# Attention of groups 4 to 6 one weight pair sooner, K's logarithms and exponentials in one row, and x's split held behind them

## The chip, the cores and the metric

One core of a Trainium2 chip runs the whole program in one launch. The metric is the device time in microseconds (us); lower is better. The names used below: TensorE (PE in the rows; PEld is its weight loads), VectorE (DVE), ScalarE (ACT), GpSimd (POOL), and SyncE, whose queue issues most DMAs (SPq). A few DMAs are issued from ScalarE's queue (ACTq).

## The reference

A complex linear recurrence over 768 steps, for 4 x 8 heads of 48 channels, gives the rows `x` of a mixture of four experts with ReLU; every expert sees every row.

```python
def _attn_ref(q, k, v, a_re, a_im):
    mag = np.sqrt(a_re * a_re + a_im * a_im)
    scale = np.minimum(mag, 0.999) / (mag + 1e-06)
    a_re_n, a_im_n = (a_re * scale, a_im * scale)
    for t in range(S):
        ar, ai = (a_re_n[:, :, t, :, None], a_im_n[:, :, t, :, None])
        new_re = ar * S_re - ai * S_im
        new_im = ar * S_im + ai * S_re
        kv = np.einsum('bhd,bhe->bhde', k[:, :, t], v[:, :, t])
        S_re, S_im = (new_re + kv, new_im)
        y[:, :, t] = np.einsum('bhd,bhde->bhe', q[:, :, t], S_re)
...
def _moe_ref(x, domain_probs, w1, w2):        # x: 3072 x 384, F = 1024
    p = domain_probs / (domain_probs.sum(-1, keepdims=True) + 1e-09)
    for e in range(E):
        h = np.maximum(x @ w1[e], 0.0)
        out += p[:, e:e + 1] * (h @ w2[e])
```

## The kernel before

The 3072 rows are cut into 12 groups of 256. For each group the program first normalises the decays A (`norm`: squares, a reduction, a logarithm, an exponential and some products), multiplies them up along time (`prefix`, a scan whose last rows are L376 and L377), and then makes Q and K. `head` (L487 to L508) squares the scanned A (L488, L489), reduces (L492), takes logarithm (L494) and exponential (L495) of the two token halves, and multiplies Q (L497). `tail` (L512 to L516) multiplies K. Q and K go through DRAM (`q_d`, `k_d`) into another layout (Qst, Kst), TensorE makes scores (`sc`) and `yp`, ScalarE copies `y`, and a store from ScalarE's queue puts it in DRAM (`y_d`, L704). `load_x` (L218) brings it back as `xa`.

Ahead of an expert, `split_x` (L221) cuts `xa` into a rounded high part `xha` (ScalarE, L225) and a low part `xla` (VectorE, L227). `moe1(g-1)` runs experts 0 and 1 on one group: eight weight pairs, each with a `w1_step` of 18 matmuls into `ph` (L238), ScalarE's ReLU `hh` (L249), VectorE's remainder `hl` (L250), and a `w2_step` of 12 matmuls into `po` (L261). The work of pair k stands in the names as `ph_k`, `hh_k`, `hl_k`. After the last pair of an expert, ScalarE adds `po` into `acc` (two instructions, one for each 128 rows, L743).

Below, block g is the stretch in which TensorE runs `moe1` on group g. In block g the attention of group g+1 is spread between the pairs, and `norm`, `prefix` and `head` of the groups behind it too. `stream` (L884) hands out that work in portions, `between(k)` (at L940) is called after pair k: from pair `FIRST` on it issues three steps of attention, and at the last pair it calls `split_x` for the next group (L948). `FIRST` (L60), `STEP` and `MORE` are tables written by hand.

What each engine runs is a fixed row of instructions. The scheduler of the program sets it when the program is built, by a simulated timeline; `behind(x, p)` makes x stand behind p there, and `keep_in_program_order` fixes an instruction's place among others so marked. At run time an engine works through its row from the front.

After the twelve groups a second phase runs experts 2 and 3 on other tiles. Its weights (`late_weights`) are prepared at the end of the first phase, with stores `late_d` from SyncE's queue (L793, L794).

Of the kernel before, what the change touches and what calls it, by code (L numbers as in the profile page):

```python
# [11 lines left out]
ALU = mybir.AluOpType  # L12
# [44 lines left out]
NSEL = 2  # L57
XSEL = 3
NPIN = 5
FIRST = {1: 5, 2: 5, 3: 4, 4: 4, 5: 4, 6: 4, 7: 3, 8: 3, 9: 3, 10: 3, 11: 3}  # L60
STEP = {1: 4.2, 2: 4.2, 3: 4.2, 4: 4.2, 5: 4.2}
MORE = (1.9, 1.9, 0.5)
HALF = tuple(range(2, 12))
# [59 lines left out]
def fast_path(ctx, tc, qkP, aP, vP, probsP, w, out, flag):  # L123
# [94 lines left out]
        wts["xd"] = nc.sync.dma_start(x, y_d[g].rearrange("(j p) t -> p j t", p=P))  # L218
        return [(slice(0, G), x)]

    def split_x(g, parts):  # L221
        xh = moe.tile([P, NJ, G], F32R, tag="xh", name=f"xha{g}")
        xl = moe.tile([P, NJ, G], F32R, tag="xl", name=f"xla{g}")
        for ts, x in parts:
            ins = nc.scalar.activation(xh[:, :, ts], x, AF.Copy)  # L225
            tc.keep_in_program_order(ins)
            tc.keep_in_program_order(nc.vector.tensor_tensor(xl[:, :, ts], x, xh[:, :, ts], op=ALU.subtract))  # L227
        wts["x"] = ins
        return xh, xl

# [65 lines left out]
    with ExitStack() as c1:  # L296
# [165 lines left out]
        def finish(g, A, qk):  # L462
# [24 lines left out]
            def head(lo, hi):  # L487
                nc.scalar.activation(some(a2a, lo, hi), some(A[:, 0], lo, hi), AF.Square)  # L488
                nc.scalar.activation(some(b2a, lo, hi), some(A[:, 1], lo, hi), AF.Square)  # L489
                for c in range(lo, hi):  # L490
                    a2, ic = some(a2a, c, c + 1), some(i0a, c, c + 1)
                    red = nc.vector.tensor_tensor_reduce(a2, a2, some(b2a, c, c + 1), scale=1.0, scalar=3e38,  # L492
                                                         op0=ALU.add, op1=ALU.min, accum_out=st_a2[:, c, g:g + 1])
                    nc.scalar.activation(ic, a2, AF.Ln, scale=2.0 ** A2_LOG[c], bias=a2b)  # L494
                    last_act = nc.scalar.activation(ic, ic, AF.Exp, scale=-1.0, bias=a2e[:, c:c + 1])  # L495
                for c in range(2):
                    ins = nc.vector.tensor_tensor(dst(Q[:, c, :, :C], lo, hi), rows(A[:, c], lo, hi),  # L497
                                                  rows(qk[:, 0], lo, hi), op=ALU.mult)
                    if g < NSEL and lo == 1:
                        behind(ins, red)  # L500
                        last["qp"] = ins
                if hi == CG:
                    nc.scalar.activation(Q[:, :, :, C].rearrange("p c (j n) -> p c j n", n=CG),
                                         A[:, :, SEG - 1, NS - 1::NS].unsqueeze(3).broadcast_to([P, 2, NJ, CG]),
                                         AF.Copy)
                return last_act
# [381 lines left out]
        def stream():  # L888
            for g in range(1, NG):
                if g > NSEL:  # L890
                    here = nc.sync.dma_start(here_d, Kst[0:1, 0, CG - 1, 0:1])
                    behind(here, last["q"])
                    last["q"] = here
                qk = load_qk(g, last["q"])
                if g + 1 < NG:
                    A.append(load_a(g + 1, prev=last["q"]))
                for r in front(g, A[g], qk):
                    yield g, r
                if g + 1 < NG:
                    for r in norm(g + 1, A[g + 1]):  # L900
                        yield g, r

        work = stream()
# [20 lines left out]
        for g in range(1, NG + 1):  # L924
# [7 lines left out]
            def between(k, g=g, first=first, end=end):  # L932
# [12 lines left out]
                    if k == end:  # L945
                        over.add(g)
                if k == max(end, nk - 1) and g in x and g >= NSEL:
                    x[g] = split_x(g, x[g])  # L948
                advance(STEP.get(g, 3.4) + (MORE[k - first] if first <= k <= end else 0.0), g + 1)

            moe1(g - 1, *x.pop(g - 1), between)
# [565 lines left out]
```

## Time and profile before

| | |
|---|---|
| time, median of 3 runs | 964.38 us (963.53 to 966.71) |
| the profiled execution's own time | 963.93 us |
| its span, first to last instruction | 962.2 us |
| TensorE busy | 935.6 us (97%) |
| VectorE busy | 740.6 us (77%) |
| ScalarE busy | 480.2 us (50%) |
| mean granted TensorE clock | 0.997 |

A busy share is a mean over all stages. A timeline row gives start and length of one instruction or of several alike that follow each other, and in brackets how long the engine stood idle ahead of it, with the instruction that it waited for. Lengths of neighbours overlap by a pipelining share, so that the distance of two starts is the price of an instruction in a row. A released wait names what came last.

### The profile page before, as it was taken

The page shows a single profiled execution, that of the slowest core. Times are in us where ns is not written, and L with a number is a line of the kernel's source. Part 1 is how long each engine was busy: PE and PEld are TensorE (multiplying, and loading weights), DVE is VectorE, ACT ScalarE, POOL GpSimd, SP SyncE. Part 2 cuts the span into 40 slices and gives each one's busy share as a digit, 9 for nine tenths or more (in the row PEclk, how much of TensorE's full clock was granted, in tenths as well). Part 3 has the DMA queues.
Part 4 walks back from the last instruction along what each step waited for, and adds up shares of the span by engine and source line. Part 5 has one row for each costly group of instructions (what it writes and reads, how often), then busy time and mean ns, then how long its engine had stood idle before and what let it go on. Part 6 is the DMA issues. An engine that isn't in the chain of part 4 may idle for free.

```text
span 962.2 us, 18383 instructions
## 1 busy us (share of the span) xinstructions
PE 935.6 (97%) x7037; PEld 912.9 (95%) x7037; DVE 740.6 (77%) x1640; ACT 480.2 (50%) x952; POOL 165.2 (17%) x206
## 2 busy tenths in 40 slices
PE   5899999999999999999999999999999999999997
PEld 3799999989999999999999999999999999999997
DVE  7889989988989999889895676758485757676642
ACT  7756436364464636446253455636454554444430
POOL 6020000000000000000000026333534362322000
PEclk9999999999999999999999999999999999999999
DMA  9686175674857468393949799231514443131112
GB/s 299 193 156 165 54 202 137 166 150 135 179 149 187 120 149 192 113 216 97 215 115 275 268 302 273 60 116 41 151 60 137 155 96 99 50 99 50 50 50 77
DMA packets 131459, 139.57 MB, mean 145 GB/s; under 512 B 8802, under 2 KB 115090, under 8 KB 131362
## 3 DMA queue, kind: packets, MB, share of 16 engines
q1 hardware_dynamic: 116130, 107.84, 38.9%
q0 software_dynamic: 11488, 26.93, 12.1%
q10 hardware_dynamic: 3744, 3.54, 1.4%
q8 instruction: 57, 0.93, 0.4%
q14 instruction: 40, 0.33, 0.1%
HBM read 89.80 MB, written 48.47 MB: 144 GB/s over the span
## 4 chain that ended last, share of the span: by engine, by line
PE 60%; DMA 3%; DVE 2%; ACT 1%; issue 0%; SPq 0%; DVEq 0%; ACTq 0%
PE pob L979 20%; PE pb L979 17%; PE po L261 9%; PE ph L238 9%; PE sc L604 2%; PE yp L621 1%; PE yp L626 1%; DMA RX<-w 1%; PE dp L586 1%; DMA Z<-y_d 1%; PE ktp L567 1%; DMA late_d<-lwl 0%; DMA xa<-y_d 0%; DVE lws L779 0%; DMA y_d<-y 0%
## 5 line engine op out<-in xcount | busy, mean ns | idle before, releaser
L979 PE MATMUL pob<-shi,hid 128*128 128x384 f32 x528 | 148.3, 334 | 0.0
L261 PE MATMUL po<-whi,hh 128*128 128x384 f32 x384 | 129.9, 338 | 1.4 <-ACT hh L249 1.0
L261 PE MATMUL po<-wlo,hh 128*128 128x384 f32 x384 | 128.7, 335 | 0.0
L249 ACT ACTIVATE hh<-ph 128x512 fp32r<-128x512 f32 x96 | 57.1, 595 | 132.0 <-PE ph L238 126.2
L991 POOL TENSOR_TENSOR Z<-Z 128x384 f32<-128x384 f32 x84 | 90.6, 1123 | 112.3 <-DMA Z<-y_d 47.9
L238 PE MATMUL ph<-xha,whi 128*128 128x256 f32 x576 | 103.3, 287 | 2.9 <-ACT xha L225 2.8
L238 PE MATMUL ph<-xla,whi 128*128 128x256 f32 x576 | 101.8, 284 | 0.6 <-DVE xla L227 0.6
L238 PE MATMUL ph<-xha,wlo 128*128 128x256 f32 x576 | 102.4, 284 | 0.0
L979 PE MATMUL pb<-xh,shi 128*128 128x384 f32 x291 | 97.2, 335 | 0.6 <-DVE pb L985 0.6
L979 PEld LDWEIGHTS pob<-shi,hid 128*128 128x128 f32 x528 | 96.4, 188 | 0.2 <-DVE hid L988 0.2
L979 PE MATMUL pb<-xh,slo 128*128 128x384 f32 x288 | 96.2, 334 | 0.0
L979 PE MATMUL pb<-xl,shi 128*128 128x384 f32 x288 | 96.2, 334 | 0.0
L250 DVE SCALAR_TENSOR_TENSOR hl<-ph,hh 128x512 fp32r<-128x512 f32 x96 | 66.0, 688 | 32.3 <-ACT hh L249 31.8
L238 PEld LDWEIGHTS ph<-xha,whi 128*128 128x128 f32 x576 | 85.1, 190 | 5.4 <-ACT xha L225 4.0
L979 PE MATMUL pob<-slo,hid 128*128 128x384 f32 x264 | 88.2, 334 | 0.0
L261 PE MATMUL po<-whi,hl 128*128 128x384 f32 x384 | 84.3, 336 | 0.0
L238 PEld LDWEIGHTS ph<-xla,whi 128*128 128x128 f32 x576 | 83.2, 190 | 1.1 <-DVE xla L227 0.8
L238 PEld LDWEIGHTS ph<-xha,wlo 128*128 128x128 f32 x576 | 82.7, 190 | 0.2 <-issue 0.2
L982 ACT ACTIVATE SN<-pb 128x384 f32<-128x384 f32 x96 | 47.3, 492 | 66.6 <-PE pb L979 59.2
L985 DVE TENSOR_TENSOR xl<-Z,xh 128x384 fp32r<-128x384 f32 x104 | 60.1, 607 | 21.1 <-ACT xh L982 13.3
L261 PEld LDWEIGHTS po<-whi,hh 128*128 128x128 f32 x384 | 72.4, 189 | 2.2 <-ACT hh L249 1.4
L982 ACT ACTIVATE hid<-pb 128x384 fp32r<-128x384 f32 x76 | 37.3, 490 | 72.3 <-PE pb L979 71.7
(227 smaller groups left out, 2069.6 us busy)
## 6 DMA issues: line engine op xcount, KB each, us to landing
qk<-qkP SPq DMA_DIRECT2D x24, 384.0 KB, 3.6
acc_d<-acc POOLq DMA_DIRECT2D x24, 384.0 KB, 4.8
ACC<-acc_d SPq DMA_DIRECT2D x48, 192.0 KB, 2.9
A<-aP SPq DMA_DIRECT2D x22, 384.0 KB, 5.5
k_d<-K SPq DMA_DIRECT2D x40, 192.0 KB, 4.1
Kst<-k_d SPq DMA_DIRECT2D x40, 192.0 KB, 5.7
Z<-y_d SPq DMA_DIRECT2D x16, 384.0 KB, 3.9
q_d<-Q SPq DMA_DIRECT2D x24, 193.5 KB, 3.7
```

The lines of the kernel that those rows point to most:

```text
L238: ins = nc.tensor.matmul(ph[:, u, :], wt[:, j * P:(j + 1) * P], xt[:, j, :], start=(n == 0), stop=(n == 3 * NJ - 1))
L249: wts["hh"] = nc.scalar.activation(hh, ph, AF.Relu)
L250: wts["hl"] = nc.vector.scalar_tensor_tensor(hl, ph, 0.0, hh, op0=ALU.max, op1=ALU.subtract)
L261: ins = nc.tensor.matmul(po[t], part[0][:, u, t * P:(t + 1) * P], wts[i][n][:, HD:], start=(i % FE == 0 and part[0] is hh and n == 0), sto ...
L567: ins = nc.tensor.transpose(kt_ps[:, j * P:(j + 1) * P], K[0][:, i, j * CG + c, :], ident)
L586: ins = nc.tensor.matmul(d_ps[o:o + n, h, :], KT[:, h, o:o + n], vc[:, h * D:(h + 1) * D], start=True, stop=True)
L604: ins = nc.tensor.matmul(s_ps[:, h, :], Kc[:, hf * 4 + h, :], Qc[:, hf * 4 + h, :], start=True, stop=True)
L621: ins = nc.tensor.matmul(yo, st[:, o:o + n], Qc[:, o // D, :], start=True, stop=False)
L979: return tc.keep_in_program_order(nc.tensor.matmul(*args, **kw))
L982: return pin(nc.scalar.activation(dst, src, fn, scale=scale))
L985: pin(nc.vector.tensor_tensor(dst, x, y, op=op))
L991: nc.gpsimd.tensor_tensor(dst, x, y, op=op)
```

## The change

Four things are changed. `FIRST` goes from 4 to 3 for groups 4, 5 and 6. In `head`, for groups above 2, the logarithm of the second half is held behind the exponential of the first, so that exponential, logarithm and exponential stand in one row. The norm of the next group (its squares and its reduction) is held behind the last exponential and the last K product for these groups. And `split_x` for groups from 3 on is held: `xha` behind the last exponential, `xla` behind the last Q product that have been issued.

```diff
--- before.py
+++ after.py
@@ -57,7 +57,7 @@
 NSEL = 2
 XSEL = 3
 NPIN = 5
-FIRST = {1: 5, 2: 5, 3: 4, 4: 4, 5: 4, 6: 4, 7: 3, 8: 3, 9: 3, 10: 3, 11: 3}
+FIRST = {1: 5, 2: 5, 3: 4, 4: 3, 5: 3, 6: 3, 7: 3, 8: 3, 9: 3, 10: 3, 11: 3}
 STEP = {1: 4.2, 2: 4.2, 3: 4.2, 4: 4.2, 5: 4.2}
 MORE = (1.9, 1.9, 0.5)
 HALF = tuple(range(2, 12))
@@ -218,13 +218,16 @@
         wts["xd"] = nc.sync.dma_start(x, y_d[g].rearrange("(j p) t -> p j t", p=P))
         return [(slice(0, G), x)]
 
-    def split_x(g, parts):
+    def split_x(g, parts, prev=(None, None)):
         xh = moe.tile([P, NJ, G], F32R, tag="xh", name=f"xha{g}")
         xl = moe.tile([P, NJ, G], F32R, tag="xl", name=f"xla{g}")
         for ts, x in parts:
             ins = nc.scalar.activation(xh[:, :, ts], x, AF.Copy)
             tc.keep_in_program_order(ins)
-            tc.keep_in_program_order(nc.vector.tensor_tensor(xl[:, :, ts], x, xh[:, :, ts], op=ALU.subtract))
+            low = tc.keep_in_program_order(nc.vector.tensor_tensor(xl[:, :, ts], x, xh[:, :, ts], op=ALU.subtract))
+            for later, p in zip((ins, low), prev):
+                if p is not None:
+                    behind(later, p)
         wts["x"] = ins
         return xh, xl
 
@@ -491,11 +494,14 @@
                     a2, ic = some(a2a, c, c + 1), some(i0a, c, c + 1)
                     red = nc.vector.tensor_tensor_reduce(a2, a2, some(b2a, c, c + 1), scale=1.0, scalar=3e38,
                                                          op0=ALU.add, op1=ALU.min, accum_out=st_a2[:, c, g:g + 1])
-                    nc.scalar.activation(ic, a2, AF.Ln, scale=2.0 ** A2_LOG[c], bias=a2b)
+                    ln = nc.scalar.activation(ic, a2, AF.Ln, scale=2.0 ** A2_LOG[c], bias=a2b)
+                    if g > NSEL and c > lo:
+                        behind(ln, last_act)
                     last_act = nc.scalar.activation(ic, ic, AF.Exp, scale=-1.0, bias=a2e[:, c:c + 1])
                 for c in range(2):
                     ins = nc.vector.tensor_tensor(dst(Q[:, c, :, :C], lo, hi), rows(A[:, c], lo, hi),
                                                   rows(qk[:, 0], lo, hi), op=ALU.mult)
+                    last["qm"] = ins
                     if g < NSEL and lo == 1:
                         behind(ins, red)
                         last["qp"] = ins
@@ -897,7 +903,8 @@
                 for r in front(g, A[g], qk):
                     yield g, r
                 if g + 1 < NG:
-                    for r in norm(g + 1, A[g + 1]):
+                    prev = (last["act"], last["dve"]) if g > NSEL else (None, None)
+                    for r in norm(g + 1, A[g + 1], prev=prev):
                         yield g, r
 
         work = stream()
@@ -945,7 +952,7 @@
                     if k == end:
                         over.add(g)
                 if k == max(end, nk - 1) and g in x and g >= NSEL:
-                    x[g] = split_x(g, x[g])
+                    x[g] = split_x(g, x[g], (last["act"], last["qm"]) if g >= XSEL else (None, None))
                 advance(STEP.get(g, 3.4) + (MORE[k - first] if first <= k <= end else 0.0), g + 1)
 
             moe1(g - 1, *x.pop(g - 1), between)
```

The rows of the engines are the same in both kernels up to the middle of block 2. The first place shown is ScalarE at the border of block 2 and block 3. Here `xha_2417` is the split of group 3, `A_1530` group 4's decays and `A_2003` group 5's, `s`, `u` the intermediates of `head` and `norm`, `acc_1` the sum of block 2. Before:

```order
L249 ACTIVATE hh_6_2401<-ph_6_2382 128x512
L225 ACTIVATE xha_2417<-xa_2354 128x768
L249 ACTIVATE hh_7_2462<-ph_7_2443 128x512
L488 ACTIVATE s_2006<-A_1530 128x768
L489 ACTIVATE s_2006<-A_1530 128x768
L494 ACTIVATE u_2007<-s_2006,a2b 128x24x16
L503 ACTIVATE Q_2008<-A_1530 128x12
L389 ACTIVATE s_2430<-A_2003 128x768
L390 ACTIVATE s_2430<-A_2003 128x768
L249 ACTIVATE hh_0_2516<-ph_0_2497 128x512
L494 ACTIVATE u_2007<-s_2006,a2b 128x24x16
L495 ACTIVATE u_2007<-u_2007,a2e 128x24x16
```

After:

```order
L252 ACTIVATE hh_6_2401<-ph_6_2382 128x512
L252 ACTIVATE hh_7_2462<-ph_7_2443 128x512
L749 ACTIVATE acc_1_2532<-po_4_0_2208,pr 128x384
L749 ACTIVATE acc_1_2532<-po_4_1_2209,pr 128x384
L491 ACTIVATE s_2006<-A_1530 128x768
L492 ACTIVATE s_2006<-A_1530 128x768
L497 ACTIVATE u_2007<-s_2006,a2b 128x24x16
L509 ACTIVATE Q_2008<-A_1530 128x12
L500 ACTIVATE u_2007<-u_2007,a2e 128x24x16
L497 ACTIVATE u_2007<-s_2006,a2b 128x24x16
L500 ACTIVATE u_2007<-u_2007,a2e 128x24x16
L225 ACTIVATE xha_2417<-xa_2354 128x768
```

`xha` moved from behind `hh_6` to behind the two copies into `acc_1` and the whole row of group 4's `head`; `hh_7` now stands ahead of it. The squares of group 5's norm (`s_2430`) come behind it.

The second place is TensorE at the same border. `po_4` is the sum that `acc_1` copies, `whi` and `wlo` are weights. Before:

```order
L261 MATMUL po_4_0_2208<-whi_602,hl_6_2402 128x384
L261 MATMUL po_4_1_2209<-whi_602,hl_6_2402 128x384
L238 MATMUL ph_0_2497<-xha_2417,whi_502 128x256 x3
L238 MATMUL ph_0_2497<-xha_2417,wlo_503 128x256 x3
L261 MATMUL po_4_0_2208<-whi_604,hh_7_2462 128x384
L261 MATMUL po_4_0_2208<-wlo_824,hh_7_2462 128x384
L261 MATMUL po_4_1_2209<-whi_604,hh_7_2462 128x384
```

After (the fence leaves out the rest of pair 7's twelve matmuls):

```order
L264 MATMUL po_4_0_2208<-whi_602,hl_6_2402 128x384
L264 MATMUL po_4_1_2209<-whi_602,hl_6_2402 128x384
L264 MATMUL po_4_0_2208<-whi_604,hh_7_2462 128x384
...
L264 MATMUL po_4_0_2208<-whi_606,hl_7_2463 128x384
L264 MATMUL po_4_1_2209<-whi_606,hl_7_2463 128x384
L241 MATMUL ph_0_2497<-xha_2417,whi_502 128x256 x3
L241 MATMUL ph_0_2497<-xha_2417,wlo_503 128x256 x3
L241 MATMUL ph_1_2554<-xha_2417,whi_524 128x256 x3
L241 MATMUL ph_1_2554<-xha_2417,wlo_525 128x256 x3
L241 MATMUL ph_0_2497<-xla_2418,whi_502 128x256 x3
```

All twelve matmuls of pair 7's `w2_step` moved ahead of the first matmul that reads `xha`, and the first ones of `ph_1` moved up among those of `ph_0`. Behind the last `po_4` row nothing stands that does not read `xha` or `xla`.

The third place is ScalarE at the next border, of block 3 and block 4, with the split of group 4 (`xha_2981` before, `xha_3003` after). Before:

```order
L488 ACTIVATE s_2486<-A_2003 128x768
L249 ACTIVATE hh_6_2965<-ph_6_2946 128x512
L489 ACTIVATE s_2486<-A_2003 128x768
L225 ACTIVATE xha_2981<-xa_2918 128x768
L494 ACTIVATE u_2487<-s_2486,a2b 128x24x16
L503 ACTIVATE Q_2488<-A_2003 128x12
L389 ACTIVATE s_2994<-A_2483 128x768
L390 ACTIVATE s_2994<-A_2483 128x768
L494 ACTIVATE u_2487<-s_2486,a2b 128x24x16
L495 ACTIVATE u_2487<-u_2487,a2e 128x24x16
L249 ACTIVATE hh_7_3026<-ph_7_3007 128x512
L495 ACTIVATE u_2487<-u_2487,a2e 128x24x16
```

After:

```order
L252 ACTIVATE hh_5_2930<-ph_5_2911 128x512
L491 ACTIVATE s_2486<-A_2003 128x768
L492 ACTIVATE s_2486<-A_2003 128x768
L497 ACTIVATE u_2487<-s_2486,a2b 128x24x16
L509 ACTIVATE Q_2488<-A_2003 128x12
L252 ACTIVATE hh_6_2987<-ph_6_2968 128x512
L500 ACTIVATE u_2487<-u_2487,a2e 128x24x16
L497 ACTIVATE u_2487<-s_2486,a2b 128x24x16
L500 ACTIVATE u_2487<-u_2487,a2e 128x24x16
L392 ACTIVATE s_2955<-A_2483 128x768
L393 ACTIVATE s_2955<-A_2483 128x768
L225 ACTIVATE xha_3003<-xa_2883 128x768
```

Here `head` of group 5 starts ahead of `hh_6` and not around it, `xha` stands behind the exponentials and behind the squares of the next norm, and `hh_7` follows it; the copies into `acc` come later. TensorE keeps its order of the row before here: six matmuls that read `xha`, then pair 7's `po`. The borders up to that of blocks 8 and 9 look like this one, with `hh_6` up to three places earlier in the row of `head` at four of them.

At the border of blocks 10 and 11 TensorE now has eight of pair 7's `po` matmuls ahead of the first six that read `xha`, the last step of group 11's attention stands inside `ph_6` where it stood behind pair 3's `po`, and on SyncE's queue the load of `xa` stands behind the first two stores of `late_d` (L794) where it stood ahead of them.

## Rows read from the trace of the kernel before

**Rows 1.** The page's first part: TensorE's busy time, its share of the span and its instructions.

```profile
PE 935.6 (97%) x7037; PEld 912.9 (95%) x7037; DVE 740.6 (77%) x1640; ACT 480.2 (50%) x952; POOL 165.2 (17%) x206
```

**Rows 2.** The view of waits, TensorE alone: who waited for whom, microseconds in total, times, the longest.

```profile
PE qp L457 <- DVE Q L497: 2.8, 1, 2.8
PE ph L238 <- ACT xha L225: 2.8, 3, 1.6
```

**Rows 3.** The timeline of TensorE around the border of block 2 and block 3 (start us, length us, line, operation, tiles; in brackets the idle time before it and who ended it).

```profile
188.28 0.52 PE L238 MATMUL ph<-xha,whi 128*128 128x256 f32 x3
190.43 0.34 PE L261 MATMUL po<-whi,hh 128*128 128x384 f32 x1
191.82 0.86 PE L261 MATMUL po<-whi,hl 128*128 128x384 f32 x4
194.27 0.62 PE L238 MATMUL ph<-xha,whi 128*128 128x256 f32 x3 [1.59 <-ACT xha L225]
```

**Rows 4.** The timeline of ScalarE over the same border, same columns.

```profile
193.38 0.84 ACT L225 ACTIVATE xha<-xa 128x768 fp32r<-128x768 f32 x1 [4.92 <-DMA xa<-y_d]
194.13 0.58 ACT L249 ACTIVATE hh<-ph 128x512 fp32r<-128x512 f32 x1
194.60 0.84 ACT L488 ACTIVATE s<-A 128x768 f32<-128x768 f32 x1
195.34 0.83 ACT L489 ACTIVATE s<-A 128x768 f32<-128x768 f32 x1
196.81 0.62 ACT L494 ACTIVATE u<-s,a2b 128x384 f32<-128x384 f32 x1 [0.64 <-DVE st_a L492]
197.43 0.83 ACT L389 ACTIVATE s<-A 128x768 f32<-128x768 f32 x1
198.17 0.83 ACT L390 ACTIVATE s<-A 128x768 f32<-128x768 f32 x1
199.39 0.60 ACT L494 ACTIVATE u<-s,a2b 128x384 f32<-128x384 f32 x1
199.89 0.61 ACT L495 ACTIVATE u<-u,a2e 128x384 f32<-128x384 f32 x1
200.40 1.03 ACT L743 ACTIVATE acc<-po,pr 128x384 f32<-128x384 f32 x2
```

**Rows 5.** The timeline of VectorE, same columns: the reduction of group 4's norm, K of group 3, the end of group 4's norm, the last scan row of group 4, and the last scan row of group 5.

```profile
157.98 0.95 DVE L391 CUSTOM_DVE_ANT_0 s<-s 128x768 f32<-128x768 f32 x1
164.21 1.02 DVE L516 TENSOR_TENSOR K<-A,u 128x384 f32<-128x384 f32 x2
167.72 1.76 DVE L418 TENSOR_TENSOR A<-A,s 128x1536 f32<-128x1536 f32 x1
190.40 0.83 DVE L377 TENSOR_TENSOR A<-fm_1a,fm_1b 128x651 f32<-128x651 f32 x1
233.31 0.83 DVE L377 TENSOR_TENSOR A<-fm_1a,fm_1b 128x651 f32<-128x651 f32 x1
```

**Rows 6.** The view by windows (stretch, its length, busy time and count of PE, PEld, DVE, ACT, POOL, then the granted TensorE clock as a share, DMA share, GB/s) for the stretch after TensorE's wait for `qp`, the border, and the end of the program; below it the last matmul row of TensorE's timeline.

```profile
27.00:28.00 1.00, 0.84 (x10) 0.78 (x12) 0.95 (x5) 0.90 (x2) 0.00 (x0) 0.94 1.18 415
28.00:30.00 2.00, 2.00 (x22) 1.98 (x19) 2.00 (x7) 0.39 (x2) 0.00 (x0) 0.50 0.83 290
30.00:32.00 2.00, 2.00 (x17) 1.67 (x14) 2.00 (x6) 0.71 (x2) 0.00 (x0) 0.68 0.01 3
192.00:194.00 2.00, 0.68 (x4) 0.36 (x3) 0.37 (x1) 0.62 (x1) 0.00 (x0) 1.00 0.37 130
959.00:960.00 1.00, 0.00 (x0) 0.00 (x0) 0.00 (x0) 0.00 (x0) 0.00 (x0) 0.86 0.05 11
960.00:962.00 2.00, 0.00 (x0) 0.00 (x0) 0.00 (x0) 0.00 (x0) 0.00 (x0) 0.50 0.02 8
...
955.42 0.34 PE L979 MATMUL pob<-shi,hid 128*128 128x384 f32 x1
```

**Rows 7.** The timeline of TensorE at three more places in the attention blocks.

```profile
241.95 0.52 PE L238 MATMUL ph<-xla,whi 128*128 128x256 f32 x3
243.14 0.45 PE L261 MATMUL po<-whi,hh 128*128 128x384 f32 x1 [0.67 <-ACT hh L249]
329.31 0.51 PE L238 MATMUL ph<-xha,wlo 128*128 128x256 f32 x3
330.16 0.44 PE L261 MATMUL po<-whi,hh 128*128 128x384 f32 x1 [0.34 <-ACT hh L249]
342.22 0.86 PE L261 MATMUL po<-whi,hl 128*128 128x384 f32 x4
343.19 0.57 PE L604 MATMUL sc<-Qst,Kst 112*128 112x128 f32 x3
```

**Rows 8.** The timelines of ScalarE, of SyncE's DMA issues and of TensorE at the border of blocks 10 and 11: the last `y` of group 11 and its split, `xa`'s load and one store of the late weights, and block 11's first `ph`.

```profile
537.64 1.21 ACT L632 ACTIVATE y<-yp 48x512 f32<-48x512 f32 x2 [1.03 <-PE yp L626]
544.75 0.85 ACT L225 ACTIVATE xha<-xa 128x768 fp32r<-128x768 f32 x1
541.51 0.37 SPq L218 DMA_DIRECT2D xa<-y_d  x1
545.35 0.32 SPq L794 DMA_DIRECT2D late_d<-lwm  x1
550.54 0.62 PE L238 MATMUL ph<-xha,whi 128*128 128x256 f32 x3
```

## Prediction

> **What bounds the kernel now.** I read the busy shares first [rows 1]: TensorE works for 935.6 of 962.2 us, so a change pays only where it takes idle time from TensorE, and costs only where it adds some. Then the view of waits for TensorE alone [rows 2]. Among the waits on other engines after the start-up, the largest entry is `ph` waiting for `xha`: 2.8 us in three waits, and one of them, 1.6 us, is at the border of blocks 2 and 3. So I went to the timelines of that border.
>
> TensorE ends pair 6 of block 2 (the four `hl` matmuls that start at 191.82, with 0.173 us between starts, so the next could start at 192.51) and then stands until `xha` lets it start at 194.27 [rows 3]. The two starts are 1.76 us too far apart; that is the whole price of the wait, restart included. ScalarE shows why [rows 4]: `xha` starts at 193.38 after 4.92 us of idle time that `xa`'s load ends. The next row shows something else: `hh` of pair 7 runs at 194.13, right behind `xha`, though its `ph` was complete when TensorE began the following `po` matmuls at 190.43 [rows 3]. It was ready for over 3 us on an idle engine, and did not pass the `xha` ahead of it. So ScalarE's row holds at run time, and what stands ahead of `xha` in that row is paid in full.
>
> **The change part by part.** *The split of group 3.* In the changed row, `xha` of group 3 stands behind `hh_7`, the two copies into `acc_1` and the whole `head` of group 4. The copies read the sum of block 2, which is complete only when pair 7's last `hl` matmul is. So all of `head` must run after block 2's last matmul and ahead of block 3's first, and TensorE has nothing else queued there. Step by step:
>
> TensorE: pair 7's twelve `po` matmuls follow pair 6 at once, and a `w2_step` lasts 2.09 us (from 190.43 to 192.51) [rows 3]. Block 2 ends at 192.51 + 2.09 = 194.6.
>
> ScalarE: two copies, 1.03 us [rows 4], to about 195.65. Then the start of L488 to the start of the first logarithm, 2.21 us (194.60 to 196.81, with the reduction between them) [rows 4]. That logarithm and the small Q copy take 0.62 (196.81 to 197.43), and the exponential, logarithm and exponential 0.5 each (199.39 to 199.89 to 200.40) [rows 4]. `xha` thus starts at 195.65 + 2.21 + 0.62 + 1.5 = 200.0, and with its own 0.84 it ends at 200.8. From the order alone TensorE is idle from 194.6 to 200.8, 6.2 us.
>
> VectorE can only add to it. `head` needs the last scan row of group 4, which before starts at 190.40 [rows 5] and ends at 191.2. The scan now starts later: the reduction of group 4's norm, at 157.98 before, is held behind K of group 3, which ends at 165.2 [rows 5]. K comes 0.9 us sooner without that reduction ahead of it, so the reduction is up to 6.3 us later. The old way from there to the norm's last product at 167.72 has K's rows in it (the last two alone 0.9 us [rows 5]) that are now done, so I carry 4 to 5.4 us to the scan's end: 195.2 to 196.6. At the lower end the copies are later still and the idle time stays at 6.2 us; at the upper end it is 7.2. I take 6.6.
>
> With a restart of 0.16 (1.76 against the 1.59 of idle time that the row prints [rows 3]) the new wait is 6.8 us, and the old 1.76 goes: **+5.0 us**, with ends +4.6 and +5.6. `xla`, which stands behind three of K's products on VectorE, may add 0 to 0.3.
>
> *The clock behind it.* TensorE's granted clock is 1.00 through the wait of 1.59 us [rows 6], so that wait cost nothing further. After the wait of 2.8 us for `qp` [rows 2] the clock falls at about 27.9 to half (1.2 of 2.4 GHz) and is back at about 31.3, 3.4 us later [rows 6]. At the end, with the last matmul at 955.42 and nothing behind it, the clock reads full until about 959.7 and then half [rows 6]. An idle time of 6.6 us is longer than that, so I expect it to fall within the gap and the first matmuls of block 3 to run at half speed. I take 3.4 to 4 us of them, half of it lost: **+1.8 us**; ends 0 (no fall) and 2.1. At half speed the wait for `xla` is covered.
>
> The Trainium skill, page "TensorE: Matmul & The Clock Gate", section "HAM oscillation — how this bites in real kernels", says that a TensorE left waiting between bursts starts the next burst throttled, and gives 1.67 us of throttled time for each burst of its example, half of which is lost. By that figure the term would be an estimated 0.8 us and the sum 1.0 us lower. The row here measures the stretch at half clock as twice as long, and that is the one I use.
>
> *The later borders.* There the copies stand behind `xha`. From the end of `ph_6` TensorE has `po` of pair 5, `ph_7` and `po` of pair 6 ahead of it, 2.09 + 2.15 + 2.09 = 6.3 us [rows 3]. ScalarE's longest row from that point is `hh_6`, logarithm, Q copy, exponential, logarithm, exponential (2.6 us), the two squares (0.74 each [rows 4]) and `xha` (0.84), 4.9 us. So `xha` is in time by 1.4 us if the squares of `head` are done by then. At the first such border pair 6 ended at 243.14 - 0.83 - 2.15 = 240.2 before (the wait below and one `ph`) [rows 7]; 6.8 later for the new wait and 6.3 back, `ph_6` ends near 240.7. The scan of group 5 ended at 234.1 before [rows 5]; with the held norm I place it near 236, and the squares with their reduction 2.2 us behind that. The cover holds, and it grows, since `FIRST` puts the attention one pair (4.2 us) ahead.
>
> What this frees is read at three places where TensorE stood for ScalarE or for Kst in blocks 4 to 6 [rows 7]. A full `ph` row of three matmuls lasts 0.36, so 243.14 comes 0.83 too late after 241.95, and 330.16 comes 0.49 too late after 329.31; four `po` last 0.69, so 343.19 comes 0.28 too late. That is 1.6 us: **-1.6 us**, with ends 0 (each reappears elsewhere in the new row) and -2.1 (two more gaps of about 0.2).
>
> *The last border.* Group 11's attention ends about one pair later (4.2 us and some), and on SyncE's queue `xa`'s load is moved past two stores of late weights. Before, `xa` was issued at 541.51, `xha` ended at 545.6, and block 11's first `ph` started at 550.54 [rows 8], a slack of 4.9 us. TensorE's own order gives another 1.4 us (eight `po` matmuls go ahead). `y` is then late by 4.7 us with 6.3 to spend. The store that now stands ahead of `xa` was issued at 545.35 [rows 8], about when `y` lands in the new order. I cost it at nothing; if the store is later too, it costs up to 2 us.
>
> *The rest.* `FIRST` for three groups and the row of logarithms move work within engines that have idle time; no instruction is added. I cost them at nothing beyond the terms above.
>
> Sum, against the profiled execution's own time of 963.93 us: 963.93 + 5.0 + 1.8 - 1.6 = **969.1 us**. Its own time lies 0.45 us under the median of 964.38, which is inside the range.
>
> **The rivals.**
>
> *The clock does not fall.* For it: the fall at 27.9 came when TensorE had already resumed after a wait and had been half idle for some time, so that row doesn't prove that one gap does it; against it: the end of the program, where idle time alone did. Time: 963.93 + 5.0 + 0.3 - 1.6 = 967.6; with the low ends (4.6, and -2.1) 966.4, which a measurement couldn't tell from no change.
>
> *A second border comes late.* At the border of blocks 3 and 4 `head` stands ahead of `hh_6` now, so a late scan would hold `hh_6` and then `xha`; at blocks 10 and 11 it is the queue. For it: the slack of 1.4 us on ScalarE and some 1.5 us on SyncE's queue are both small. Against it: VectorE needs less than a block for a group, so the scan gains from block to block. A miss of 2 us, without another fall of the clock, gives 971.1; with one, 973.
>
> *Faster: the hold is free.* If block 2's copies and `head` ran before TensorE's row ended, the old wait of 1.76 us and the 1.6 us at the other places would go and nothing would come: 963.93 - 1.76 - 1.6 = 960.6. It decides at one point: `xha` of group 3 ends ahead of 194.6. For it: `hh_7` comes sooner by 3 us, and VectorE has spare time. Against it: the copies stand ahead of `head` in ScalarE's row, and `hh` at 194.13 shows that nothing passes there.
>
> *The change moves next to nothing.* All holds fall where the engines waited anyway: about 964. Against it stands the same row.
>
> **How the numbers follow.** Forecast (one long wait at blocks 2 and 3, clock at half behind it): 0.66, 968 to 970.5. A second late border: 0.15, 970.5 to 973. No fall of the clock: 0.14, 966 to 968. Hold free or gains larger than I see: 0.03, 960.6. Next to nothing: 0.02, 964. The range from 966.3 to 972.5 leaves out the last two, and the ends of the second and third case.
>
> A measurement of this kernel can tell about 0.3% from no change, 2.9 us: slower is over 967.3, faster under 961.5. Slower: 0.66 + 0.15 + half of 0.14 = 0.88, less a little for terms missed, 0.86. Same: 0.11. Faster: 0.03.
>
> **What would show it.** In the changed profile, the wait of `ph` for `xha` at about 194.6 should read 6 to 7 us, with two copies, `head`'s two squares, logarithm, exponential, logarithm and exponential ahead of `xha` on ScalarE's timeline; the granted clock should read 0.5 for 3 to 4 us from about 201, in windows of 2 us; the waits of `po` for `hh` in the waits view should be gone or under 0.5 us; and `ph` should not wait for `xha` again up to 586 us. I am wrong if `xha` of group 3 runs before the copies, if the wait is under 4 us, or if the clock stays at full level.

## The result, and the profile after

The changed kernel takes 973.21 us (median of 6 runs, 971.71 to 974.75) against 964.87 us for the kernel before in the same session (6 runs). The ratio is 1.0084, 95% interval 1.0069 to 1.0100: slower by 8.3 us, where I had forecast 5.2 and a range up to 972.5. The direction was right and the size was not. The profiled execution took 973.38 us, with a span of 971.6.

First the busy shares and then the waits of TensorE in the changed kernel, to be read beside [rows 1, 2]: busy time has hardly moved, so the time is in gaps.

```profile
PE 936.2 (96%) x7037; PEld 912.7 (94%) x7037; DVE 741.0 (76%) x1640; ACT 479.1 (49%) x952; POOL 165.0 (17%) x206
```

```profile
PE ph L241 <- ACT xha L225: 9.1, 5, 6.7
PE qp L460 <- DVE Q L502: 3.1, 1, 3.1
PE po L264 <- DVE hl L253: 1.3, 2, 1.0
PE sc L610 <- issue: 1.1, 1, 1.1
PE po L264 <- ACT acc L749: 0.5, 1, 0.5
```

The wait for `xha` went from 2.8 us to 9.1, and three smaller entries are of a kind that the first did not lead me to expect. TensorE's timeline at the border of blocks 2 and 3, to set beside [rows 3]:

```profile
193.62 0.86 PE L264 MATMUL po<-whi,hl 128*128 128x384 f32 x4
201.22 1.01 PE L241 MATMUL ph<-xha,whi 128*128 128x256 f32 x3 [6.75 <-ACT xha L225]
202.03 0.84 PE L241 MATMUL ph<-xha,wlo 128*128 128x256 f32 x3
203.95 0.60 PE L241 MATMUL ph<-xla,whi 128*128 128x256 f32 x3
204.38 0.52 PE L241 MATMUL ph<-xha,whi 128*128 128x256 f32 x3
```

The last of the four `po` starts at 194.14, the next matmul at 201.22: 7.08 us, 6.91 more than the usual 0.17. ScalarE's timeline over that gap, beside [rows 4]:

```profile
194.34 1.05 ACT L749 ACTIVATE acc<-po,pr 128x384 f32<-128x384 f32 x2 [3.39 <-PE po L264]
195.80 0.84 ACT L491 ACTIVATE s<-A 128x768 f32<-128x768 f32 x1 [0.41 <-DVE A L379]
198.02 0.61 ACT L497 ACTIVATE u<-s,a2b 128x384 f32<-128x384 f32 x1 [0.63 <-DVE st_a L495]
199.82 0.61 ACT L500 ACTIVATE u<-u,a2e 128x384 f32<-128x384 f32 x1
200.34 0.83 ACT L225 ACTIVATE xha<-xa 128x768 fp32r<-128x768 f32 x1
```

The two copies, the squares, the logarithms and the exponentials stand between block 2's last matmul and `xha`, in the order that the prediction read from the code. The windows of this stretch (columns as in [rows 6]):

```profile
196.00:198.00 2.00, 0.00 (x0) 0.00 (x0) 1.09 (x4) 1.39 (x2) 0.54 (x1) 0.82 0.62 58
198.00:200.00 2.00, 0.00 (x0) 0.00 (x0) 2.00 (x4) 1.95 (x5) 0.00 (x0) 0.50 0.75 138
202.00:204.00 2.00, 2.00 (x12) 2.00 (x11) 2.00 (x5) 0.64 (x1) 0.00 (x0) 0.50 0.95 247
204.00:206.00 2.00, 2.00 (x18) 2.00 (x18) 2.00 (x5) 0.35 (x1) 0.00 (x0) 0.97 0.36 104
```

The granted clock falls near 197.3 (0.82 over the two microseconds from 196) to 0.50, the 1.2 GHz level, and is back just behind 204. Of that, 2.9 us (201.22 to about 204.1) fall on matmuls, and half of it, some 1.4 us, is lost.

So far this is the forecast. The rest lies at the other end of the first phase. Timelines of VectorE, SyncE's DMA issues, ScalarE and TensorE there, beside [rows 8]: the last scan row of group 11, the last load of its `Kst`, its first `sc`, a store of late weights, `xa`'s load and split, block 11's first `ph`, a wait for `hl`, and the first matmul of the second phase:

```profile
500.71 0.83 DVE L380 TENSOR_TENSOR A<-fm_1a,fm_1b 128x651 f32<-128x651 f32 x1
529.41 1.23 SPq L539 DMA_DIRECT2D Kst<-k_d  x2
533.41 2.02 PE L610 MATMUL sc<-Qst,Kst 112*128 112x128 f32 x16 [1.10 <-issue]
550.77 0.32 SPq L800 DMA_DIRECT2D late_d<-lwm  x1
555.35 0.37 SPq L218 DMA_DIRECT2D xa<-y_d  x1
558.73 0.84 ACT L225 ACTIVATE xha<-xa 128x768 fp32r<-128x768 f32 x1 [3.14 <-DMA xa<-y_d]
559.62 0.62 PE L241 MATMUL ph<-xha,whi 128*128 128x256 f32 x3 [0.85 <-ACT xha L225]
571.52 0.97 PE L264 MATMUL po<-whi,hl 128*128 128x384 f32 x4 [1.00 <-DVE hl L253]
594.97 0.33 PE L986 MATMUL pb<-xh,shi 128*128 128x384 f32 x1
```

In the kernel before, the scan row starts at 486.25, the `sc` at 520.38, `xa`'s load at 541.51, and the second phase at 585.26. To see where the time accrues I compared TensorE's start of the same matmul in both traces. At the last `po` of block 9 the changed kernel is 3.3 us late, with six `ktp` matmuls (0.57 us) still to do that the other had behind it, so 3.9 on equal work. At the first matmul of the second phase it is 9.7 us late, and it stays so to the last matmul (+9.67). **Some 5.8 us, more than the whole net forecast of 5.2, is lost within blocks 10 and 11**, in small pieces: 1.26 at the `sc`, about 0.2 at each of five `yp`, 0.41 at `scs`, 1.01 at `xha`, 1.17 and 0.47 at `hl`, 0.67 at `acc` (start to start, less the usual step; a piece of 0.60 was there before).

### The profile page after: what moved, and what is told of

It is laid out like the page before. It is cut to its first block, busy times and chain, and to the rows that moved or that the text cites. A ratio compares the mean times of both kernels' runs of the same rounds, so it can differ in the third digit from the quotient of the medians.

```text
span 971.6 us, 18406 instructions
## 1 busy us (share of the span) xinstructions
PE 936.2 (96%) x7037; PEld 912.7 (94%) x7037; DVE 741.0 (76%) x1640; ACT 479.1 (49%) x952; POOL 165.0 (17%) x206
## 4 chain that ended last, share of the span: by engine, by line
PE 83%; DVE 8%; ACT 3%; DMA 2%; issue 1%; SPq 1%; DVEq 0%; ACTq 0%
PE pob L986 20%; PE ph L241 18%; PE pb L986 17%; PE po L264 16%; PE sc L610 4%; PE yp L632 2%; PE dp L592 2%; PE yp L627 2%; PE ktp L573 1%; PE xp L662 1%; DMA late_d<-lwm 1%; DVE hl L253 1%; DMA late_d<-lwl 1%; DMA Z<-y_d 1%; SPq L539 1%
```

## The experiments

"Lost in blocks 10 and 11" below is the growth of that lateness from the last `po` of block 9 to the second phase, on equal work. What each theory says stands in the expectations.

**e1: the kernel before with the three `FIRST` entries alone.**

```diff
-FIRST = {1: 5, 2: 5, 3: 4, 4: 4, 5: 4, 6: 4, 7: 3, 8: 3, 9: 3, 10: 3, 11: 3}
+FIRST = {1: 5, 2: 5, 3: 4, 4: 3, 5: 3, 6: 3, 7: 3, 8: 3, 9: 3, 10: 3, 11: 3}
```

> Only the three entries of FIRST are changed, no hold. Theory one (the long wait at blocks 2 and 3 is the split's hold, the loss of 6.4 us between block 10 and the second phase is the norm's hold, FIRST pays): the wait of ph for xha at the border of blocks 2 and 3 is 1.6 us as before, the second phase starts no later than before, and the time is 962 to 964.5 us, about 1 to 3 us under the kernel before. Theory two (FIRST pushes the end of the first phase): the second phase starts 4 us or more later than before's 585.3 and the time is over 967.

Measured: 964.42 us, ratio 0.9999 (0.9988 to 1.0010). Nothing is gained and nothing lost; block 3's `sc` now starts 1.13 us too late, for loads that aren't there yet. `FIRST` alone brings no gain, and the loss at the end isn't its work.

**e2: the change without the hold on `xha` and `xla`.**

```diff
-                    x[g] = split_x(g, x[g], (last["act"], last["qm"]) if g >= XSEL else (None, None))
+                    x[g] = split_x(g, x[g], (None, None))
```

> The changed kernel without the hold on the split (xha, xla free); FIRST, the row of logarithms and the norm's hold stay. Theory one: the wait at the border of blocks 2 and 3 is 2 us or less and the clock stays at full level there, which takes away 6.5 us, while the loss at the end of the first phase stays at 6 us or grows, since the norm's hold is still there: 966 to 970 us. Theory two (the split's hold makes the end late too): the end's loss is under 1.5 us and the time is 961 to 963.

Measured: 994.24 us, 1.0302 (1.0285 to 1.0319), 24 us beyond every expectation. The wait at blocks 2 and 3 is only 0.66 us, but `xha` is late by 0.5 to 1.2 us at nearly every later border, and the last border costs eleven. Two rows of TensorE:

```profile
565.71 0.67 PE L627 MATMUL yp<-Qst,G 112*48 112x128 f32 x4 [4.82 <-DVE G L603]
581.55 1.01 PE L241 MATMUL ph<-xha,whi 128*128 128x256 f32 x3 [11.56 <-ACT xha L225]
```

So with the split free the harm at the end is larger and not smaller: it belongs to the hold on the norm, which stands here beside `FIRST` and the row of logarithms. The last scan row starts at 523.4, 37 us later than before. In this kernel the loop from K of a group through the next group's held norm, scan and `head` to the next K takes 46.1 us on average (the last scan rows of groups 5 to 11 are 43.3 to 48.7 apart), and a block takes about 44.4 in the kernel before: nothing can catch up. Not all of this is waiting: the granted clock is 0.50 from about 564 to 584.5, some 7 us of TensorE's work fall into that, and an estimated 3.5 us of them are the clock's. That the split's hold shortens this loop (44.2 us in the changed kernel), by forcing `head` ahead, is argued and not shown.

**e3: the change without the hold on the norm.**

```diff
-                    prev = (last["act"], last["dve"]) if g > NSEL else (None, None)
+                    prev = (None, None)
```

> The changed kernel without the hold on the next group's norm; FIRST, the row of logarithms and the split's hold stay. Theory one: the wait at the border of blocks 2 and 3 is still 6 to 7.5 us (the norm's squares now stand ahead of xha too) with a stretch of half clock behind it, and the loss at the end of the first phase is gone: 966 to 968 us. Theory two: the end's loss stays and the time is 972 to 974.

Measured: 971.92 us, 1.0071 (1.0054 to 1.0088). TensorE's rows at the border and at the second phase, and the clock in the window of the border:

```profile
200.20 1.01 PE L241 MATMUL ph<-xha,whi 128*128 128x256 f32 x3 [5.11 <-ACT xha L225]
...
591.67 0.34 PE L986 MATMUL pb<-xh,shi 128*128 128x384 f32 x1
```

```profile
200.00:202.00 2.00, 1.80 (x8) 1.80 (x9) 2.00 (x5) 0.97 (x2) 0.00 (x0) 0.50 0.74 123
```

The loss in blocks 10 and 11 is 0.3 us instead of 5.8 (6.1 us late at block 9, 6.4 at the second phase): the expected sign of the cause. The time is 4 us above the expectation all the same: the first wait stays at 5.1 us with the clock at half behind it, since the norm's squares now stand in ScalarE's row between `head` and the copies; less comes back in blocks 4 to 9; and the span ends 8.7 us after the last matmul instead of 6.8, which I can't explain.

**e4: the two holds and the row of logarithms, with `FIRST` as before.**

```diff
-FIRST = {1: 5, 2: 5, 3: 4, 4: 3, 5: 3, 6: 3, 7: 3, 8: 3, 9: 3, 10: 3, 11: 3}
+FIRST = {1: 5, 2: 5, 3: 4, 4: 4, 5: 4, 6: 4, 7: 3, 8: 3, 9: 3, 10: 3, 11: 3}
```

> The changed kernel with FIRST as before (4 for groups 4, 5 and 6), all holds in place. Theory one: the wait of 6 to 7 us at blocks 2 and 3 and the end's loss are both there, and what blocks 4 to 9 gave back (3 us) is less: 973 to 976 us. If the holds themselves give that gain, the time stays at 972.5 to 973.5; if FIRST is what makes the long wait, the wait is under 3 us and the time under 970.

Measured: 974.81 us, 1.0105 (1.0082 to 1.0128). The first wait is the same 6.75 us, and blocks 10 and 11 lose 4.7. In between, on equal work, the lateness goes from 6.9 us just behind the first wait to 5.5 at the end of block 9: 1.4 us come back without any `FIRST`, against 2.2 (6.1 to 3.9) in the changed kernel. The difference is about as much as one `sc` of block 6 starts too late here (348.40, 0.76 us start to start), which it doesn't there. So the holds make the loss and the larger part of the gain; beside them `FIRST` adds some 0.8 us to the gain, read from one trace of each kernel.

**e5: the change with TensorE kept busy in the gap**, by 46 matmuls behind block 2's last `po`, whose result isn't read.

```diff
                     w2_step(f2, hh, hl, po, wts.pop(("hold", b, f2), ()))
+                    if b == 2 and f2 == NF1 // 2 - 1:
+                        dm = wts["pool"].tile([P, G], F32, tag="pa", name="dm")
+                        for _ in range(46):
+                            ins = nc.tensor.matmul(dm, wts[0][0][:, :P], xh[:, 0, :], start=True, stop=True)
+                            behind(ins, wts["po"])
```

> The changed kernel with 46 matmuls of 256 columns into an unused sum (their result is not read) right behind block 2's last matmul, so that TensorE works through most of the wait for group 3's split. Theory one: xha still lets block 3 start at 201.2 us (within 0.3), TensorE's idle time there falls from 6.7 to 1 to 2 us, the granted clock stays at 1.00, the first twelve matmuls take 1.45 us where they took 2.73, and the time falls by 1.2 to 1.5 us against the changed kernel, to about 971.8 us. Rival: the stretch at half clock does not come from the idle time; it stays, and so does the time of 973.2 us.

Measured: 974.81 us, 1.0096 (1.0071 to 1.0121). Rows of TensorE, and the window that was at half clock:

```profile
194.23 5.67 PE L297 MATMUL dm<-xha,whi 128*128 128x256 f32 x46
201.15 0.62 PE L241 MATMUL ph<-xha,whi 128*128 128x256 f32 x3 [1.26 <-ACT xha L225]
...
572.27 0.98 PE L264 MATMUL po<-whi,hl 128*128 128x384 f32 x4 [2.26 <-DVE hl L253]
```

```profile
202.00:204.00 2.00, 1.91 (x17) 1.71 (x16) 2.00 (x5) 0.57 (x1) 0.00 (x0) 1.00 0.94 237
```

The clock stays at 1.00, and block 3's first twelve matmuls take 1.78 us instead of 2.73, so the clock term is real and 0.9 to 1.0 us could be had back. It is kept up to block 9 (2.35 us late against 3.3) and gone at the second phase (10.45 against 9.7). It is still there when group 11's attention runs: the last scan row starts 1.0 us sooner (499.7) and `sc` 1.7 us sooner (531.73). It goes behind that, where TensorE waits 0.91 us for `scs`, 1.36 for `xha` and 2.26 for `hl`; in the changed kernel these waits are 0.25, 0.85 and 1.00.

**e6: the norm's hold left out for groups 9 to 11.**

```diff
-                    prev = (last["act"], last["dve"]) if g > NSEL else (None, None)
+                    prev = (last["act"], last["dve"]) if NSEL < g < 8 else (None, None)
```

> The changed kernel with the norm's hold only for the norms of groups 4 to 8; those of groups 9, 10 and 11 are free. Theory one (the hold makes each group's attention a chain as long as a TensorE block, so that group 11's comes late and drags the late weights and the second phase): the wait of 6.9 us and the half clock stay, blocks 3 to 7 are as in the changed kernel, the scan of group 11 ends 8 us or more earlier against its block, and the second phase starts no more than 1.5 us later against block 9's end than before: 966.5 to 968.5 us. Rival (the end is late because of the split's hold or of the lateness of all before it): the loss of 6 us at the end stays and the time is over 971.

Measured: 969.59 us, 1.0050 (1.0037 to 1.0064), a microsecond over the expectation. The loss in blocks 10 and 11 falls from 5.8 to 1.4 us, most of it one wait of `sc` (rows of VectorE and TensorE):

```profile
492.65 0.83 DVE L380 TENSOR_TENSOR A<-fm_1a,fm_1b 128x651 f32<-128x651 f32 x1
525.06 1.16 PE L610 MATMUL sc<-Qst,Kst 112*128 112x128 f32 x8 [1.08 <-DMA Kst<-k_d]
590.10 0.33 PE L986 MATMUL pb<-xh,shi 128*128 128x384 f32 x1
```

Up to group 8 this kernel's scan runs as the changed one's does. The last scan row of group 8, in the changed kernel and here:

```profile
368.15 0.83 DVE L380 TENSOR_TENSOR A<-fm_1a,fm_1b 128x651 f32<-128x651 f32 x1
368.35 0.83 DVE L380 TENSOR_TENSOR A<-fm_1a,fm_1b 128x651 f32<-128x651 f32 x1
```

From there to group 11's it takes 132.6 us with the norm held (500.71) and 124.3 without (492.65), 44.2 against 41.4 for a group. That difference is the hold's.

**e7: no hold on the norm, and the split held from group 6 on** (`if g >= 6`, with e3's edit).

```diff
-                    x[g] = split_x(g, x[g], (last["act"], last["qm"]) if g >= XSEL else (None, None))
+                    x[g] = split_x(g, x[g], (last["act"], last["qm"]) if g >= 6 else (None, None))
```

> FIRST as changed, the row of logarithms, the split held for groups 6 to 11 only, the norm not held. Theory one (the split's hold costs only where the attention has no lead, which by group 6 it has): no wait of ph for xha above 1.8 us, no stretch of half clock, second phase within 1 us of before: 963 to 965.5 us. Rival (the split's hold costs some at every border): 967 us or more.

Measured: 966.88 us, 1.0013 (1.0002 to 1.0023), 1.4 us over the expectation. The wait at blocks 2 and 3 is 1.84 us, about as expected, but a stretch at half clock follows it, which the expectation ruled out:

```profile
194.37 0.95 PE L241 MATMUL ph<-xha,whi 128*128 128x256 f32 x3 [1.84 <-ACT xha L225]
...
194.00:196.00 2.00, 1.63 (x7) 1.63 (x8) 1.65 (x3) 2.00 (x4) 0.00 (x0) 0.62 0.00 0
196.00:198.00 2.00, 2.00 (x8) 2.00 (x8) 2.00 (x7) 1.37 (x4) 0.00 (x0) 0.53 0.00 0
```

Over it TensorE's lateness grows from 0.1 to 1.55 us. Four starts of `sc` that come 0.33 to 0.96 us too late, two of them for a load of `Kst`, add to that and waits of [rows 7] go; the second phase starts 2.65 us late.

**e8: the change with the split held from group 4 on, not 3.**

```diff
-                    x[g] = split_x(g, x[g], (last["act"], last["qm"]) if g >= XSEL else (None, None))
+                    x[g] = split_x(g, x[g], (last["act"], last["qm"]) if g > XSEL else (None, None))
```

> The changed kernel with the split held from group 4 on and not from group 3. Theory one (the first border that is held pays, wherever it is, since the attention has no lead there): the wait at blocks 2 and 3 is under 2 us, one of 7 to 9 us with half clock behind it stands at blocks 3 and 4, where now two squares of the next norm stand ahead of xha too, and the end is as late as in the changed kernel or later, since xa's load for group 11 stands behind all four stores of late weights: 974 to 984 us. Rival (only group 3 has the problem): no wait above 2 us at either border and 965 to 968 us.

Measured: 981.42 us, 1.0165 (1.0143 to 1.0187), within the expectation. The long wait only moves to the next border, again with the clock at 0.50 behind it. The end is late too, and there the clock is at 0.50 from about 564.4 to 571.3 as well:

```profile
250.59 1.01 PE L241 MATMUL ph<-xha,whi 128*128 128x256 f32 x3 [7.97 <-ACT xha L225]
...
567.91 1.01 PE L241 MATMUL ph<-xha,whi 128*128 128x256 f32 x3 [5.64 <-ACT xha L225]
```

**e9: the norm held for groups 9 to 11 alone**, the reverse of e6.

```diff
-                    prev = (last["act"], last["dve"]) if g > NSEL else (None, None)
+                    prev = (last["act"], last["dve"]) if g >= 8 else (None, None)
```

> The counterpart of the run that held the norms of groups 4 to 8: here only those of groups 9, 10 and 11 are held, with FIRST, the row of logarithms and the split's hold as in the changed kernel. Theory one (the end is late because the attention's lead, built up over the blocks, is missing by group 11): the lead built up by group 8 suffices, the second phase starts no more than 2 us later against block 9's end than before, and the time is 971 to 973 us, like the run without the norm's hold. Rival (a hold among the last three groups is what delays the late weights, lead or not): 5 us or more are lost at the end and the time is 976 or more.

Measured: 968.95 us, 1.0033 (1.0019 to 1.0047). Blocks 10 and 11 lose nothing: 5.6 us late at block 9 on equal work, 4.9 at the second phase. The last three holds alone do no harm, so the loss is not made by the holds of the groups where it shows. The five earlier ones alone make 1.4 us of it (e6), all eight 5.8. The time is 2 us below the expectation and 3 below e3; half of that lies ahead of the second phase, the other half behind the last matmul.

**e10: e5 and e6 together.** The edits are those two, and the 46 matmuls' result isn't read here either.

> The run with the norm held for groups 4 to 8, with the 46 filling matmuls at the border of blocks 2 and 3. In the run with the filling alone the microsecond gained at the border was given back at the end of the first phase, where TensorE waited for group 11's attention. Theory one (that end ran at the attention's pace, so an earlier TensorE waited longer there): with the attention in time at the end the gain stays, and the span is 0.9 to 1.4 us under the 966.6 us of the run without the filling, with the clock at full level throughout: a time of 968 to 968.9 us. Rival (the filling gains nothing by itself): span 966.2 to 967.

Measured: 969.43 us, 1.0034 (1.0023 to 1.0045), no better than e6. The clock stays up, and 0.75 us is held at block 9 against e6 (+2.67, +3.42); at the second phase the two stand at +5.21 and +4.84. It goes in block 11, in two waits for `hl`, of which this is the first:

```profile
571.65 0.96 PE L264 MATMUL po<-whi,hl 128*128 128x384 f32 x4 [0.91 <-DVE hl L253]
```

`hl` stands on VectorE behind the second phase's first work on `Z`. The second of its two loads landed 6.3 us after its issue here (560.14 to 566.4) and 3.4 us after it in e6 (560.04 to 563.4). Why that load took longer stays open.

**e11: the kernel before with `FIRST` of groups 5 and 6 alone.**

```diff
-FIRST = {1: 5, 2: 5, 3: 4, 4: 4, 5: 4, 6: 4, 7: 3, 8: 3, 9: 3, 10: 3, 11: 3}
+FIRST = {1: 5, 2: 5, 3: 4, 4: 4, 5: 3, 6: 3, 7: 3, 8: 3, 9: 3, 10: 3, 11: 3}
```

> The kernel before with FIRST at 3 for groups 5 and 6 only, no hold. In the run with FIRST alone TensorE waited 1.1 us in block 3 for the scores of group 4, whose Kst was not there so early. Theory one: that wait is absent with group 4 left at 4, and the waits of 0.83, 0.49 and 0.28 us in blocks 4 to 6 are partly gone: 963 to 964.5 us, up to 1.5 us under the kernel before. Rival (FIRST moves waits and removes none): 964.5 to 965.5.

Measured: 964.52 us, 0.9994 (0.9984 to 1.0004). In blocks 3, 4 and 5 matmuls start 0.88, 0.47 and 0.74 us too late, where the kernel before has 0.83, 0.49 and 0.28 in blocks 3 to 6: the waits move, and their sum doesn't shrink. No version beat the kernel before.

The runs side by side (from the timelines of VectorE and TensorE; "late" is against the kernel before, on equal work):

| kernel | last scan row of group 11, us | its first `sc`, us | late at end of block 9 | late at second phase | lost between |
|---|---|---|---|---|---|
| before | 486.2 | 520.4 | 0 | 0 | 0 |
| e1, `FIRST` only | 483.2 | 521.4 | 1.0 | 0.9 | -0.1 |
| e11, `FIRST` of 5 and 6 | 482.9 | 520.9 | 0.5 | 0.2 | -0.3 |
| e7, split held from 6, no norm hold | 485.5 | 523.5 | 3.1 | 2.7 | -0.4 |
| e3, no norm hold | 480.2 | 527.1 | 6.1 | 6.4 | 0.3 |
| e9, norm held for 9 to 11 | 486.9 | 526.1 | 5.6 | 4.9 | -0.7 |
| e6, norm held for 4 to 8 | 492.6 | 525.1 | 3.4 | 4.8 | 1.4 |
| e10, e6 with fill | 491.8 | 524.0 | 2.7 | 5.2 | 2.5 |
| e5, after with fill | 499.7 | 531.7 | 2.9 | 10.5 | 7.5 |
| after | 500.7 | 533.4 | 3.9 | 9.7 | 5.8 |
| e4, holds only | 503.9 | 533.7 | 5.5 | 10.2 | 4.7 |
| e8, split held from 4 | 505.0 | 536.5 | 7.7 | 16.6 | 9.0 |
| e2, no split hold | 523.4 | 550.6 | 9.6 | 32.2 | 22.5 |

The loss goes with the start of that scan row. Up to 487 it is 0.3 us at most, around 492 it is 1.4 to 2.5, from 499.7 to 505 it is 4.7 to 9.0, at 523 it is 22.5; in e8 and e2 a part of it is the clock's. The start is this late where the norm is held in all eight groups; neither TensorE's clock (e5) nor `FIRST` (e4) makes it so.

## Why the prediction was right and wrong

- **The border of blocks 2 and 3: right.** 6.91 us against 6.8, a net +5.15 against +5.0. The scan of group 4 ends at 196.5 (195.2 to 196.6 forecast), `xha` starts at 200.34 (200.0). Reading a row that the engine keeps, and adding the durations in it, was enough.
- **The clock: right in kind, a little smaller.** Some 1.4 us against 1.8: it fell within the gap as said, and 2.9 us of matmuls ran at half where I took 3.4 to 4. The figure of the Trainium skill, page "TensorE: Matmul & The Clock Gate", section "HAM oscillation — how this bites in real kernels" (1.67 us for each burst), lies below the 2.9 us measured here. The rival without a fall is out; e5 shows that idle time is the cause, since the fall goes with it.
- **The later borders: the places right, the size more than forecast, the reason wrong in the main.** The waits of [rows 7] are gone (2.05 us of start-to-start excess in blocks 3 to 6), some 0.8 us is new further on, and the lateness shrinks from 6.1 us just behind the first border to 3.9 by block 9, 2.2 against 1.6. I put that down to `FIRST`. e1 has `FIRST` and none of it, and e4 gives back 1.4 without `FIRST`: the larger part comes with the holds, and `FIRST` adds to it only beside them. That the long wait gives ScalarE and VectorE the time is argued. About 1 us of the 2.2 I can't place in single rows.
- **The last border: the step that failed.** "I cost it at nothing", with 2 us at most for the queue, and "the rest" at nothing, rested on the sentence that VectorE needs less than a block for a group, so that the scan gains from block to block. That was read from the kernel before, where it is so: from group 5 to group 11 its scan rows are 42.2 us apart on average and gain on a block of 44.4 each time. The held norm, which is part of the change, takes that margin away. The reduction can't run until K of the group before is done, so K, norm, scan, `head` and the next K become one chain, and in the changed trace the same scan rows are 42.3 to 45.1 us apart, 44.2 on average, where a block takes 44.2. What the kernel before saves up, 14 us of lead by group 11, is never saved. I let `y` be late by 4.7 us; its last store was issued 11.2 us late (550.04, before 538.88). Then `xa` and the second phase's loads come late one after another, and `ph` does wait for `xha` again (0.85 us at 559.62), which I had ruled out. This is +5.8 us where I had 0.
- **What is shown and what is argued.** That the norm's hold makes the loss is shown by e3. That the holds of the early groups alone make 1.4 us of it, and those of the late ones alone none, is shown by e6 and e9, that TensorE's own lateness doesn't make it by e5. That the hold lengthens the loop is shown by e6 against the changed kernel, 41.4 and 44.2 us a group from the same start. How the late scan becomes 5.8 us in blocks 10 and 11 is read from the rows; the pieces within block 11 hang on landing times that differ between runs (e5, e10), and are not settled. One rival no run tests: in the five kernels that lose 4.7 us or more, `xa`'s load stands on SyncE's queue behind two or all of the last four stores of late weights, in the others ahead of them. In the changed trace that place doesn't hold the load itself. The stores were issued by 551.1, and SyncE then stood until `y`'s last store had landed, 5.3 us after its issue where it took 2.6 before; whether stores of late weights slowed it stays open.

The sum with measured terms: 6.1 just behind the first border (5.15 and 1.4, less some 0.4, of which 0.28 is a lead that TensorE had when it came there), - 2.2 and + 5.8 make 9.7 us, the lateness of the last matmul. The rival on the late side, "a second border comes late", named the right place with the wrong mechanism (SyncE's queue, at most 2 us plus the clock). The queue did have the stores ahead of `xa` (the second at 550.77, `xa` at 555.35), but `sc` of group 11 was late 20 us before that.

## What to carry over

An instruction that is held behind another group's work can cost nothing at the place where it stands and still join two chains into one: before costing a hold at nothing, walk round the loop from group to group once and set its length against the time of a block, and not the engine's busy share. A lead that the kernel before builds up is a property of its order and no reserve that the changed one may count on. And time saved on TensorE ahead of such an end need not be kept: in e5 and e10 the 0.9 and 0.75 us of clock were gone at the second phase.

## What the hardware showed that I had not expected

- Idle time alone brought the clock down within a gap: full speed when TensorE stopped at about 194.5, half from about 197.3 on, while the wait lasted 6.75 us; in e3 a wait of 5.11 us did the same. After work resumed at 201.22 the clock was back at about 204.1.
- The length of one wait doesn't tell whether the clock falls. In e7 a wait of 1.84 us was followed by a fall (half from about 194.5 to 197.9), and one of 1.59 us at the same place of the kernel before was not. The wait of 2.8 us for `qp` there had a fall behind it [rows 2, 6]; the same wait in e3 had none:

```profile
27.19 2.85 PE L460 MATMUL qp<-Q,wide 128*64 128x128 f32 x40 [2.82 <-DVE Q L502]
...
28.00:30.00 2.00, 2.00 (x35) 1.82 (x31) 2.00 (x6) 0.76 (x2) 0.00 (x0) 1.00 0.40 137
```

- Forty-six matmuls of 256 columns (5.67 us) in the gap kept the clock at 1.00 through the 1.26 us of idle time that was left.
- The same load, issued at nearly the same time (560.14 and 560.04), landed after 6.3 us in e10 and after 3.4 us in e6. A chain that rests on such landings at several places has an end that I couldn't forecast to a microsecond from one trace.
